# Two-layer attention stack on one NeuronCore: windowed attention moved from elementwise products on VectorE to banded matmuls on TensorE

## Chip, cores and metric

The kernel runs on one core of one Trainium2 chip. The metric is device time of the launch in microseconds (us). The kernel before takes 328.93 us, the median of two runs (328.53 and 329.33).

## What is computed

A residual stream x of 2048 tokens by 512 features (bf16) passes through four attention layers, A, B, A, B. Each is x = x + layer(layernorm(x)), with its own projections wqkv and wo; the two A layers share weights, and so do the two B layers. There are 32 heads of 16 features.

```python
# layer A: linear attention with a feature map
pq = einsum("bhsd,hdf->bhsf", q, w_phi); pk = einsum("bhsd,hdf->bhsf", k, w_phi)
phi_q = concat([softmax(pq), softmax(-pq)]); phi_k = concat([softmax(pk), softmax(-pk)])
kv = einsum("bhsf,bhsd->bhfd", phi_k, v);  z = einsum("bhsf->bhf", phi_k)
o = einsum("bhqf,bhfd->bhqd", phi_q, kv) / (einsum("bhqf,bhf->bhq", phi_q, z) + 1e-6)

# layer B: each token attends to 8 tokens of its past, 2 apart (offsets 0, 2, ..., 14)
W, dil = 8, 2
idx = pos[:, None] - (arange(W) * dil)[None, :];  mask = idx >= 0
logits = where(mask, einsum("bhsd,bhswd->bhsw", q, k[idx]) * 16 ** -0.5, -1e9)
o = einsum("bhsw,bhswd->bhsd", softmax(logits), v[idx])
```

## The kernel before

The tokens are worked in four blocks of 512 (b = 0..3), the two passes through A and B are L = 0 and 1. Stages of one (L, b) are Python methods that record small steps per engine: `s_a1` (keys, values and the kv sums of layer A), `s_a2` (queries of A), `s_a3` and `s_a4` (normalisation, output of A), `s_b1` (projections of B), `s_b2` (logits and softmax of B), `s_b3` (weighted values of B), `s_out` (output projection, residual and the next layernorm). The steps of all stages are then issued in one order written out by hand, the string `_ORDER`: each word names a thread (a stage on an engine) and takes its next step. `_CHOICE` says for each eviction of PSUM (the accumulator memory) and some others whether VectorE (DVE) or ScalarE (ACT) does it (`flex`, `copy`), and for each residual add whether DVE adds it or TensorE (PE) adds it with an identity matmul (L523) and ACT evicts (L530). `_SLOTS` gives each tile its buffer. So every engine runs a fixed queue; the DMAs are all issued by SyncE's (SP's) queue, also in that order. Each PSUM tile is one bank of 512 fp32 per partition, eight in all.

Layer B before works on features across partitions and tokens along the free axis. `prod` (L1019) multiplies Q, repeated eight times, by eight shifted windows of K: 128 by 4096 elements on DVE, four per (L, b). `lgt` (L1026) sums the 16 features of a head on PE with the 0/1 matrix `indQK`; PE takes four 32-column tiles side by side. Exp (L1033) and the denominator (`den` L1042 on PE, `rd` L1047 and L1049 on ACT) follow, then `pt` (L1054) on DVE. For the values, 16 DMAs per (L, b) copy shifted rows of V into `Vg` (L988). `pav` (L1081) multiplies them with the weights on DVE, 128 by 4096 elements, four per (L, b), and `mo` (L1090) sums them on PE with `indAV`.

Small copies of the last 16 tokens of K and V from block to block (L953, L965, L969) are on GpSimd (POOL). The `vaug` ones (L614) are there too.

PE runs in several array layouts: the whole array for projections (L520, L593, L605, L698, L927), column tiles of 32 or 64 for L1026, L1090, L714, L782 and L668, row tiles for L808, and sixteen 32x32 tiles for L900.

Of the kernel before, what the change touches and what calls it, by code (L numbers as in the profile page):

```python
# [8 lines left out]
BF16 = mybir.dt.bfloat16  # L9
# [20 lines left out]
KVW = 16 + TB  # L30
VGW = 3 * KVW + TB + 8
# [5 lines left out]
_BUFS = {"big": 8, "med": 16, "t2": 6, "ps": 8}  # L37
# [3 lines left out]
    "fold_dma": (),  # L41
    "half_k": ((0, 3), (1, 3)),
    "half_ln": (),
    "split": ((1, 2), (1, 3)),
    "v_dram": (),
    "half_mo": (),
    "rho_pad": 0,
# [10 lines left out]
av 8 i i i i i i i i i i i i 0 f 0 g e 2t 0 bs 9 h a d c 0 j k t i i j l 27 o p 3 3 d6 b 1x 1x t 1y o m 2 2 1q  # L58
1z 1x 1x q u t r 1q v x w n s 1r w 1s 4 20 y 21 1x 22 1x 23 1q 1q 1q 1q 1v 1w z 3d 3d 3d 1u 1t 25 3e 3e 3e z 5
3e 3e z z 26 10 18 18 d5 1 z 16 11 4i 15 6 1h 13 3d 3e 3e 25 25 26 18 25 18 12 26 26 28 26 26 26 26 19 12 28  # L60
2a 28 1h 18 14 12 12 1a 28 1c 3e 2g 2g 1f 2h 2h 1h 1h 1b 1i 2b 1b 1e 1d 29 2j 2k 1h 1j 1n 2r 1b 1l 2s 1b 2c 2r
1k 2s 17 2g 2g 2h 2h 1k 1k 2h 2h 2h 2h 2d 1g 2d 2d 2d 2e 2j 1m 35 36 32 2o 2o 33 2s 33 32 33 33 2r 2s 2s 1o 2o
2o 2d 2r 3a 1k 3a 1p 2p 2o 24 24 2s 24 2u 2v 35 37 2u 2u 2u 2s 2i 2w 2j 3a 2s 3a 2l 2z 2j 24 32 32 34 2m 3b 33
3d 3f 3f 2z 2z 2z 33 2f 33 33 2f 2f 2f 3a 3a 2q 2q 2q 30 3a 2n 3a 3a 2z 3e 2q 2x 35 35 b6 3b 3a 2y 31 31 31 31
3c 3c 38 3c 39 3c 3m 3f 3n 3o 3o 3o 24 24 3g 3g 3g 3f 3p 3q 3g 3g 3g 3g 3g 3r 3q 3f 3g 24 3h 3i 3i 5l 5m 5n 3p
3s 3q 3j 3k 3k 3t 3q 3p 3x 5m 3w 3u 3h 3i 3i 3q 3v 3q 3q 3y 3h 3i 3q 3i 3h 3i 3q 5l 5o 5p 5r 5m 5q 7 7 3z 3q
3i 3j 3k 5m 5l 5s 3k 7 7 5m 5m 5m 3h 3i 7g 40 5u 44 41 42 5t 5m 5m 3j 3j 7h 7i 3k 5v 5m 5w 43 7h 45 7j 45 60
3k 3k 3k 46 45 45 5y 5x 5z 61 61 48 47 47 61 49 47 4a 47 4b 62 47 4b 63 3j 4g 94 4c 45 4d 45 4e 4f 3k 45 45 61
64 63 4h 4p 65 95 7j 7j 66 4q 63 96 95 97 97 63 67 7h 63 67 69 7h 6b 4k 4k 4k 4l 4p 4r 4k 4m 4p 4p 4s 4t 7k 7n
6a 68 6c 4o 7m 50 50 4u 4u 4u 4n 4u 7l 4w 97 7o 7p 7p 7q 7s 3l 4x 7r 7r 7p 7t 7p 6o 7u 50 7r 7r 7v 6o 6j 4v 4y  # L70
4j 6o 6q 6o 4j 4z 6k 6p 6r 6j 7r 6e 6l 95 6d 95 7v 6t 6s 6f 6d 7w 6e 7z 7x 98 9b 9a 99 6g 7y 9c 6e 6j 6j 9d 9d
6u 9d 6e 6n 80 6m 9d 6h 6v 6v 9e 9h 9f 6i 9g 9f 6w 6v 6v 6w 6w 9f 9i 9f 87 88 8h 9j 9f 50 82 9j 9l 6w 6x 6x 87
87 6w 81 83 9n 6x 9k 87 8b 89 51 51 51 51 52 52 8c 8c 8e 6u 6u 6u 9m 8j 8a 8d 8c 6v 6y 3l 8f 82 9o 82 85 82 50
51 52 4z 4z 4z 9q 9q 9s 8c 6z 8g 6y 6z 9r 71 70 6y 6y 6z 6z 72 86 a0 a0 a1 73 84 8i 74 75 74 74 50 74 8i 76 8i
77 a2 76 79 53 53 54 55 54 a5 56 53 54 9v 78 76 9q 9q 76 a0 81 53 9v 9w 9p 7a 57 9v 9u a7 76 7a 9t 8j 7c 9y 54
58 59 59 59 9v 59 9x 7d 7e 5a 8j 8j 7b 7f 5c 5b 5d 5b 5b a0 8k 5e 5b 5f 8k 9z a7 5b 5f 5j 8k 8k 8l a3 5i b4 a4
b7 5h b4 b4 b4 8l 5g b5 b5 a7 b5 b5 a7 8k 8l 8j c3 8i c3 b8 c4 c4 c4 c4 a8 8m a8 a8 a8 c3 a9 a9 5k at c1 b5 a6
8m au au c1 c2 b5 c2 aw c2 c2 a8 a9 b5 b5 8n 8o 8n 8p 8m at au at at 8n 8q 8m a7 aa 8n aw 8r 8s au au au 8s 8s
8t au au 8s 8v a6 a6 8u aa 8w aa 8x 8u 8u 8u 8y ab ac ab ad a6 aa b7 8u b9 b7 c3 8y 90 92 c1 91 c1 c2 8z c2 c2
aw ay ab c2 ba ae ab af aw b0 c4 c4 b1 bc ag ag ag ag ah bc aj ak bc c1 c4 c4 bc al ax c3 ai ai ai bd b1 ai am  # L80
93 bf bi bg az bf ai am ar bf bf bg bg aq b7 bg bg bg bg bg bb an ao ag ag ap bi ag ag b1 b1 bc b2 c2 bi bn bi
bl bk as bq br br bq br br bq bq b1 br by by by by bt b3 b3 b3 b3 br be be be br br bz c5 c5 bh bj bn bn bn c5
bu c4 by by by by c6 bo by c6 c6 c5 bt bt bt bn bv c6 c6 c6 bz be bp bp bw bm bp bp c0 c0 by c6 c6 bx c0 c0 c9
c5 ca c6 cb cb cc cb cd ce cd fr fs c7 c8 c7 c8 c8 ft cc ci cf cd cg cd c7 c8 c8 fs fu c8 e2 fu ch cd e3 cd cc
cj ck e4 cd c7 c8 c8 c7 e3 e2 cm cd c8 e6 e7 fu cl cd cd cn cp co e5 e3 hb e3 cr e2 ea e9 cq hc cs e3 cs e8 e3
e3 hd eb ec e3 e3 e3 ed ct cv hc eh cs he ee cs ef cw eg ei cx ei ei cu ei cu cu cu fs cy fs fv ej cu cy d0 cz
ek d2 fw fx fz d3 cs cs fy cs cs g0 g0 g0 el ek em ek en ek d4 d1 dc g1 eo ek g2 g3 g2 dc de eo es g0 g4 dd dh
g2 g5 g2 he hc eq g6 d7 d8 d7 d7 d7 he di dc g2 dc d9 ep er hc et dn hf da db df dh dh dh hi hh hj hg hk hk hk
dj dk dl dm dm g6 g7 g9 dn dn dg ga f0 f0 hl hm hn hm ho hm ev ew f1 hk dn g8 do do hp f2 fa fc hm hq do do dp
ev ex fc gb ev f0 dp ey dn f3 f0 hm fc f4 hq ev ez fc do dp dn dq dq d6 f5 f6 dm dm eu hs gi gj gi fd gs hr fd  # L90
ht fd hu hv fd dq fe fe f5 f5 f8 f5 f9 f7 fb gk fd fe fc gn gn gp gi gi gl gm gd gd gd ge ic gf i7 i7 i9 gg i8
dr dr dt ds dr du hx hy gd dq gu dr dv gn gq gh i7 ff ia gu fb go ff fg fh fb fb eu gv gc gn i2 gr i3 hx hz hx
i7 i2 ib gv i4 hx i1 gc hw i2 i2 i5 gu i0 gu gv gv gw gt ie fg fi if i6 ie id gw if dw dx id gv gw id id ie ie
if if ig dw ff ig if ig fg fj dw e0 dw ff fg fk ie fl fm fl fn gu fl fl fp ih ih ih ih e1 ii ii ii ik ij fq dy
gt gt gt fo fo il io io io io ii im ip iq ip is ir ir ih ii in ip ip iu it ir gx ir gy gx gx gx gz gy h0 dz dz
iv gy h1 h4 gx gy h2 h4 iw iv h5 h5 h6 h7 gy h4 h3 h5 h8 h9 h7 h7 h4 h5 ha h7
# [4 lines left out]
    "0011111111111001110111111010000010010000000000000001011111101100100000110101000110000010000001110111"  # L101
    "1101011110010000110101000000000000001101011000000000100100000000000000000101111100000011011000000000"
    "0000000000001101111010000000100101011111010000011001110111000000000000000111111011101110010100101000"
    "00000000000001111001000000000000000000000000000000000000000000000000000000000001111"
)


_SLOTS = {
    "big": (
        "0123456701231231456204632073205712053720457604356704213560421356720415763215063506432506"  # L110
    ),
    "med": (
        "0123456789abcdef5837ae98eeaeae471853bc9e43cbe47199ce3185413cebf94c8f74e3581bc71931bc7f370bf9ac21584e"
        "af9c37214a0b589dec37"
    ),
    "t2": (
        "0123450123450342150132451032451032451032451302153421530421503452014520345123045130425123504321504321"
        "5043215043210451023134"
    ),
    "ps": (  # L120
# [9 lines left out]
class _Fast:  # L130

    def __init__(self, ctx, tc, A_x, A_wqkv, A_w_phi, A_wo, B_wqkv, B_wo, out):
# [16 lines left out]
        for n in ("xn", "xnT", "oT", "Eq", "rS", "kvp", "K", "QT", "Vg", "PT", "vh"):  # L149
            setattr(self, n, {})  # L150
# [1667 lines left out]
```

## Time and profile before

| what | value |
|---|---|
| device time, median of two runs | 328.93 us |
| span of the profiled execution, first to last instruction | 327.5 us |
| PE busy | 310.3 us (95%) |
| DVE busy | 302.2 us (92%) |
| ACT busy | 279.3 us (85%) |
| POOL busy | 25.3 us (8%) |
| granted PE clock | 0.998 |
| bytes moved by DMA | 35.41 MB |

The span is what one profiled execution shows between its first and last instruction; its own device time is not listed beside it, and the launch adds 1.4 us to the span when the median is taken for it (328.93 - 327.5). Matmuls overlap: a 128x512 matmul is listed with 380 ns while the next starts some 216 ns after it, so PE's busy time covers short pauses too. "PEld" is the loading of weights, which runs beside the matmuls. A group's line gives the source line, the engine, the operation, the tiles, the count, the busy time and the mean duration of one.

### The profile page before, as it was taken

Reading aid. Unit: us, or ns where it says so; the run is one execution under the profiler, and the core shown is the slowest. Engines: PE = TensorE matmul, PEld = TensorE weight load, DVE = VectorE, ACT = ScalarE, POOL = GpSimd, SP = SyncE. Lnnn points to the kernel's source line nnn. Section 1 sums busy time; section 2 is a strip of 40 time slices with the busy share of each in tenths; the row PEclk is TensorE's granted clock in tenths of the full one; section 3 lists DMA queues with packets and bytes.
Section 4 is the critical chain, followed back from the end, with each engine's and each line's share of the span. In section 5 each row is a group of like instructions: output and inputs, shape, how many; then the busy total and the mean of one; then the engine's idle time right before and its main releaser. Section 6 shows DMA issues by size and latency. Waiting matters only on the chain. (4 is left out here: it accounts for less than half of the span.)

```text
span 327.5 us, 8033 instructions
## 1 busy us (share of the span) xinstructions
PE 310.3 (95%) x3176; PEld 149.5 (46%) x3203; DVE 302.2 (92%) x439; ACT 279.3 (85%) x634; POOL 25.3 (8%) x50
## 2 busy tenths in 40 slices
PE   7999999999999999999999999979999999999873
PEld 3655456445444444443444455644544454433221
DVE  7998995998998999899999999699999999999993
ACT  5999988998888999989999999798999996676550
POOL 4000000000021003000000000000000208400000
PEclk9999999999999999999999999999999999999999
DMA  7980000004556899998750300023436977679952
GB/s 197 380 197 3 0 2 4 2 20 120 105 148 135 152 164 133 139 121 154 137 135 1 67 3 2 4 59 90 128 58 125 179 146 134 150 139 158 166 176 92
DMA packets 37388, 35.41 MB, mean 108 GB/s; under 512 B 23008, under 2 KB 32224, under 8 KB 37344
## 3 DMA queue, kind: packets, MB, share of 16 engines
q1 hardware_dynamic: 36816, 34.81, 53.6%
q8 instruction: 27, 0.44, 0.6%
q14 instruction: 17, 0.14, 0.2%
q10 hardware_dynamic: 528, 0.02, 0.1%
HBM read 10.50 MB, written 2.36 MB: 39 GB/s over the span
## 5 line engine op out<-in xcount | busy, mean ns | idle before, releaser
L927 PE MATMUL ps<-xnT,WB 128*128 128x512 bf16 x384 | 87.6, 380 | 0.5 <-DMA xnT<-xn 0.5
L1081 DVE TENSOR_TENSOR pav<-PT,Vg 128x4096 bf16<-128x4096 bf16 (+1 forms) x34 | 72.0, 2162 | 1.5 <-DMA Vg<-V 1.0
L1019 DVE TENSOR_TENSOR prod<-QT,K 128x4096 bf16<-128x4096 bf16 x32 | 72.5, 2291 | 0.3 <-ACT QT L192 0.2
L927 PEld LDWEIGHTS <-WB 128*128 128x128 bf16 x384 | 42.3, 114 | 43.3 <-issue 5.8
L520 PEld LDWEIGHTS <-oT 128*128 128x128 bf16 x256 | 23.8, 97 | 34.5 <-ACT oT L192 5.7
L192 ACT CAST oT<-ps 128x512 bf16<-128x512 f32 (+1 forms) x60 | 32.1, 587 | 8.4 <-PE ps L1090 7.1
L706 ACT ACTIVATE Eq<-ps 128x512 bf16<-128x512 f32 x64 | 34.0, 615 | 0.7 <-PE ps L698 0.6
L520 PE MATMUL ps<-WoB,oT 128*128 128x512 bf16 x122 | 32.1, 380 | 2.4 <-ACT oT L192 2.0
L599 ACT ACTIVATE Ek<-ps 128x512 bf16<-128x512 f32 x64 | 33.6, 622 | 0.4 <-PE ps L593 0.2
L698 PE MATMUL ps<-xnT,WA 128*128 128x512 bf16 x128 | 30.7, 380 | 0.6 <-DVE Eq L816 0.6
L540 ACT ACTIVATE sqd<-x 128x512 bf16<-128x512 bf16 x48 | 30.1, 643 | 1.0 <-DVE x L533 0.8
L605 PE MATMUL ps<-WA,xnT 128*128 128x512 bf16 x120 | 30.0, 380 | 0.5 <-issue 0.2
L593 PE MATMUL ps<-WA,xnT 128*128 128x512 bf16 x124 | 29.7, 380 | 0.6 <-DMA xnT<-xn 0.2
L520 PE MATMUL ps<-WoA,oT 128*128 128x512 bf16 x120 | 29.2, 380 | 0.4
L533 DVE SCALAR_TENSOR_TENSOR x<-ps,x 128x512 bf16<-128x512 f32 x38 | 25.4, 686 | 1.9 <-PE ps L520 1.7
L192 ACT CAST V<-ps 128x512 bf16<-128x512 f32 x31 | 17.5, 595 | 4.4 <-PE ps L927 4.3
L192 ACT CAST K<-ps 128x512 bf16<-128x512 f32 x31 | 17.8, 585 | 3.7 <-PE ps L927 3.3
L530 ACT ACTIVATE x<-ps 128x512 bf16<-128x512 f32 x26 | 15.1, 598 | 6.4 <-PE ps L523 6.3
L192 ACT CAST QT<-ps 128x512 bf16<-128x512 f32 x29 | 17.1, 592 | 2.5 <-PE ps L927 2.5
L651 DVE TENSOR_TENSOR Ek<-Ek,rk 128x4096 bf16<-128x4096 bf16 (+1 forms) x10 | 18.6, 1858 | 0.5 <-ACT rk L646 0.5
L593 PEld LDWEIGHTS <-xnT 128*128 128x128 bf16 x128 | 12.1, 97 | 15.4 <-DMA xnT<-xn 0.7
L446 ACT ACTIVATE xn<-x,nmr,rstd 128x512 bf16<-128x512 bf16 x23 | 18.2, 822 | 1.0 <-DVE nmr L435 0.8
(129 smaller groups left out, 433.3 us busy)
## 6 DMA issues: line engine op xcount, KB each, us to landing
Vg<-V SPq DMA_DIRECT2D x128, 131.5 KB, 4.4
Prho<-rd SPq DMA_DIRECT2D x8, 512.0 KB
x<-in_A_x_dram SPq DMA_DIRECT2D x3, 512.0 KB
WB<-in_B_wqkv_dram SPq DMA_DIRECT2D x3, 512.0 KB, 11.6
wraw<-in_A_wqkv_dram SPq DMA_DIRECT2D x4, 256.0 KB, 4.5
out_dram<-x SPq DMA_DIRECT2D x4, 256.0 KB, 2.2
out_dram<-x SPq DMA_DIRECT2D x8, 128.0 KB, 2.2
x<-in_A_x_dram SPq DMA_DIRECT2D x4, 128.0 KB
```

The costliest lines, as they stand in the source:

```text
L192: self.nc.scalar.copy(out=out, in_=in_)
L520: nc.tensor.matmul(y[:], lhsT=oT[:, c, t * P:(t + 1) * P], rhs=Wo()[:, c, :], start=(c == 0), stop=(c == NB - 1 and not onpe))
L533: nc.vector.scalar_tensor_tensor(out=xb[:, t, :], in0=T[t][:], scalar=1.0, in1=xb[:, t, :], op0=ALU.mult, op1=ALU.add, **kw)
L540: nc.scalar.activation(out=sqd[:], in_=xb[:, t, :], func=ACT.Square, accum_out=T["ss"][:, t:t + 1])
L593: nc.tensor.matmul(pk[:], lhsT=xnT[:, t, k, :], rhs=self.WA[:, k, D:2 * D], start=(k == 0), stop=(k == NB - 1))
L599: nc.scalar.activation(out=T["E"][:, t, s, :], in_=T["k", t][:], func=ACT.Exp, scale=1.0 - 2.0 * s)
L605: nc.tensor.matmul(pv[:], lhsT=xnT[:, t, k, :], rhs=self.WA[:, k, 2 * D:3 * D], start=(k == 0), stop=(k == NB - 1))
L698: nc.tensor.matmul(pq[:], lhsT=self.WA[:, k, hb * P:(hb + 1) * P], rhs=xnT[:, :, k, :], start=(k == 0), stop=(k == NB - 1))
L706: nc.scalar.activation(out=self.Eq[L, b][s][:, :, hb, :], in_=T[hb][:].rearrange("p (t i) -> p t i", t=4), func=ACT.Exp, scale=1.0 - 2.0 * s)
L927: nc.tensor.matmul(pp[:], lhsT=self.WB[:, k, i * D + c:(i + 1) * D:NB], rhs=xnT[:, :, k, :], start=(k == 0), stop=(k == NB - 1))
L1019: nc.vector.tensor_tensor(out=pr[:], in0=QT[:, c:c + 1, :].to_broadcast([P, NW, TB]), in1=win, op=ALU.mult)
L1081: nc.vector.tensor_tensor(out=pv, in0=PT[:, :, lo:lo + n].unsqueeze(1).to_broadcast([P, NB, 2, n]), in1=vw, op=ALU.mult)
```

## The change

K, Q, V of layer B get another layout, and its products and sums become matmuls over short bands of tokens. The tokens of a block are dealt out to partitions by parity, since the window's steps are 2: `xv` reads x as (block, parity r, half f, partition p), so each tile of 128 token rows holds tokens of one parity, and the window of 8 tokens becomes 8 neighbours in it.

- Q is evicted to `Qs` and scattered by eight DMAs per (L, b) into `Qbd`, in which every head pair stands block-diagonally (the rest is zero). V is projected with tokens on partitions, written to DRAM (`vwr`) and read back by eight DMAs per (L, b) into `Vbd` (`vrd`), where each group of 32 tokens has a copy with the heads block-diagonal. `Vg` and its 16 DMAs are gone.
- For each of four quarter blocks t, `sc` computes the scores of 32 keys against 40 queries of two heads per matmul (32x32 tiles, 80, 64 or 16 columns, 40 matmuls for each half f), `ex` takes the exponential of 128x640, `msk` multiplies by the band's 0/1 mask (128x1280 on DVE), `mo` makes the weighted sums (`pv`, 40, 32 or 8 columns) and the denominators (`dn`, 80, 64 or 16 columns) on 64x32 tiles, `ln` and `rd` invert the denominator on ACT, and `nrm` multiplies on DVE from PSUM into `oT`. In b = 0 the first quarter of each parity (t = 0 and 2) has no matmuls for the keys before it in `pv` and `dn`.
- Layer A takes PSUM banks in pairs (`pp`): exponentials, the eviction of `oT` and the products `mulp` work on 1024 columns in place of 512; the copies `bs` of the broadcast rho are gone.
- `_ORDER`, `_CHOICE` and `_SLOTS` are new. Identity matmuls for the residual go from 26 to 4. POOL zeroes `Qbd` and `Vbd` once at the start (four memsets of 4096 or 4608 elements per partition, ahead of the `vaug` ones) and its copies from block to block are gone.

```diff
+    def pp(self):
+        return self.psp.tile([P, 2, TB], F32, name="pp", tag=self.slot("pp"))
...
-        xv = self.A_x.rearrange("b (j p) d -> p (b j) d", p=P)
+        xv = self.A_x.rearrange("b (k f p r) d -> p (b k) r f d", f=2, p=P, r=2)
...
-            nc.scalar.activation(out=T["E"][:, t, s, :], in_=T["k", t][:], func=ACT.Exp, scale=1.0 - 2.0 * s)
+            nc.scalar.activation(out=T["E"][:, 2 * t:2 * t + 2, s, :], in_=T["k", t][:], func=ACT.Exp,
+                                 scale=1.0 - 2.0 * s)
...
-        def prod(c):
-            K, QT = self.K[L, b], self.QT[L, b]
-            T["p", c] = pr = self.big([NW, TB], "prod")
...
-        def pav(q, lo=0, n=TB):
-            Vg, PT = self.Vg[L, b], self.PT[L, b]
...
+        def qsc(r, o):
+            lo = 32 * r + DH * o
+            nc.sync.dma_start(out=self.Qbd[b % 2][lo:lo + DH, :, o, :], in_=T[0][lo:lo + DH, :, :])
+
+        def vwr(r):
...
+            dst = self.VD[L][r, 256 * b:256 * b + 256, :].rearrange("(f p) d -> p f d", p=P)
+            nc.sync.dma_start(out=dst, in_=T[2][:, 2 * r:2 * r + 2, :])
+
+        def vrd(r, c):
+            j = 0 if b else 1
+            src = self.VD[L][r, 256 * b - 32 + 32 * j:256 * b + 256, c * P:(c + 1) * P]
+            lo = c % 2 * DH
+            dst = self.Vbd[b % 2][32 * c:32 * c + 32, r, j:9, lo:lo + DH, :].rearrange("k j d e -> k j (d e)")
+            nc.sync.dma_start(out=dst, in_=src.rearrange("(j k) e -> k j e", k=32))
...
+        def mm(S, r, c, s, n, pos, K, k0, q0):
+            o = S[32 * c:32 * c + 32, r % 2, s * 80 + pos:s * 80 + pos + 1]
+            out = bass.AP(o.tensor, o.offset, [list(o.ap[0]), [WN, 2], [1, n]])
+            nc.tensor.matmul(out, lhsT=K[32 * r:32 * r + 32, c, k0:k0 + 32],
+                             rhs=Q[32 * r:32 * r + 32, c, :, q0:q0 + n],
+                             start=(s == 0), stop=(pos == 32), tile_position=(32 * r, 32 * c),
+                             skip_group_check=True)
+
+        def sc(f):
+            S = T[f] = self.pp()
+            K = self.K[L, b]
+            for s in range(4):
+                for c in range(NB):
+                    for r in (2 * f, 2 * f + 1):
+                        mm(S, r, c, s, WN if s < 3 else 32, 0, K, t * P + 32 * s, t * P + 32 * s)
...
+            for c in range(NB):
+                for r in (2 * f, 2 * f + 1):
+                    mm(S, r, c, 3, 8, 32, Kp, k0, t * P)
+
+        def ex(f):
...
+            nc.scalar.activation(out=E, in_=T[f][:, :, 0:320], func=ACT.Exp, scale=float(DH) ** -0.5,
+                                 accum_out=self.stE[:, 2 * idx + f:2 * idx + f + 1])
 
         def msk():
+            E = self.ET[L, b, t][:].rearrange("p f i s o q -> p (f i s o) q")
+            nc.vector.tensor_tensor(out=E, in0=E, in1=self.maskW[:].unsqueeze(1).to_broadcast([P, 32, WN]),
+                                    op=ALU.mult)
...
+        def pv(s, n, pos, q0):
+            E, O = self.ET[L, b, t], T["O"]
+            for i in range(2):
+                for cc in range(2):
+                    for f in range(2):
+                        for o in range(2):
+                            u = 2 * f + (cc if o == 0 else 1 - cc)
+                            e = 4 * f + 2 * i + o
+                            nc.tensor.matmul(O[32 * u:32 * u + 32, o, i * P + q0:i * P + q0 + n],
+                                             lhsT=V[64 * cc:64 * cc + 64, t // 2, s, :, e],
+                                             rhs=E[64 * cc:64 * cc + 64, f, i, (s + 3 - 4 * (t % 2)) % 4, o, pos:pos + n],
+                                             start=(q0 == 0 and pos == 0 and i == 0), stop=False,
+                                             tile_position=(64 * cc, 32 * u), skip_group_check=True)
+
+        def dn(s, n, pos, q0, last):
+            E, O = self.ET[L, b, t], T["O"]
+            for cc in range(2):
+                for f in range(2):
+                    for o in range(2):
+                        u = 2 * f + (cc if o == 0 else 1 - cc)
+                        w = O[32 * u:32 * u + 32, o, 256 + q0:257 + q0]
...
+                        nc.tensor.matmul(out, lhsT=self.oneB[64 * cc:64 * cc + 64, :, :],
+                                         rhs=E[64 * cc:64 * cc + 64, f, :, s, o, pos:pos + n],
+                                         start=False, stop=last,
+                                         tile_position=(64 * cc, 32 * u), skip_group_check=True)
...
+        def ln():
+            T["l"] = self.t2([2, 256], "lnd", F32)
+            nc.scalar.activation(out=T["l"][:], in_=T["O"][:, :, 256:512], func=ACT.Ln, bias=self.tiny_t[:, 0:1])
 
         def rd():
+            T["r"] = self.t2([2, 256], "rden")
+            nc.scalar.activation(out=T["r"][:], in_=T["l"][:], func=ACT.Exp, scale=-1.0,
                                  accum_out=self.stR[:, idx:idx + 1])
 
+        def nrm():
...
+            out = self.oT[key, b][:, :, t * P:(t + 1) * P].rearrange("p (i o) q -> p o i q", o=2)
+            nc.vector.tensor_tensor(out=out, in0=T["O"][:, :, 0:256].rearrange("p o (i q) -> p o i q", i=2),
+                                    in1=T["r"][:].rearrange("p o (i q) -> p o i q", i=2), op=ALU.mult)
...
+                for t in range(4):
+                    self.s_b2(L, b, t)
+                    self.s_b3(L, b, t)
+                self.s_out("b4_%d%d" % (L, b), "A%d" % (L + 1), b, lambda: self.WoB, L == 1)
```

Instructions per engine in the built programs, on the path that runs (the matmul rows count matmuls; each has a weight load beside it):

| | before | after |
|---|---|---|
| `prod` and `pav` on DVE, 128x4096 | 62 (and 4 of 2048) | 0 |
| `lgt`, `mo`, `den` on PE | 544 | 0 |
| `sc` on PE | 0 | 2560 |
| `pv` and `dn` on PE | 0 | 2496 and 1248 |
| changes of PE's array layout | 109 | 157 |
| all PE instructions | 6408 | 17884 |
| B's Q, K, V evictions: DVE, ACT | 5, 91 | 60, 36 |
| residual adds on DVE; identity matmuls with ACT | 38; 26 | 60; 4 |
| `ex` on ACT | 16 of 512 columns | 64 of 640 |
| `ln` and `rd` on ACT, 512 columns | 8 and 8 | 32 and 32 |
| V and Q transfers on SP | 128 | 64 (`qsc`), 16 (`vwr`), 64 (`vrd`) |

## The prediction

> **What bounds the kernel now.** I read the page first: span, busy shares, then its costliest groups and the instruction queue.
>
> ```profile
> span 327.5 us, 8033 instructions
> PE 310.3 (95%) x3176; PEld 149.5 (46%) x3203; DVE 302.2 (92%) x439; ACT 279.3 (85%) x634; POOL 25.3 (8%) x50
> q8 instruction: 27, 0.44, 0.6%
> ...
> L927 PE MATMUL ps<-xnT,WB 128*128 128x512 bf16 x384 | 87.6, 380 | 0.5 <-DMA xnT<-xn 0.5
> L1081 DVE TENSOR_TENSOR pav<-PT,Vg 128x4096 bf16<-128x4096 bf16 (+1 forms) x34 | 72.0, 2162 | 1.5 <-DMA Vg<-V 1.0
> L1019 DVE TENSOR_TENSOR prod<-QT,K 128x4096 bf16<-128x4096 bf16 x32 | 72.5, 2291 | 0.3 <-ACT QT L192 0.2
> ```
>
> PE and DVE are both over 90% and ACT is not far off. The two products of layer B are 144.5 of DVE's 302.2 us. An average hides stages, so next the busy time by stretch.
>
> ```profile
> 20.00:50.00 30.00, 29.68 (x313) 15.59 (x315) 27.77 (x48) 28.07 (x61) 0.77 (x2) 1.00 0.10 22
> 110.00:140.00 30.00, 29.90 (x209) 13.71 (x212) 28.60 (x24) 27.55 (x65) 3.04 (x3) 1.00 1.02 144
> 290.00:328.00 38.00, 27.50 (x225) 9.69 (x221) 31.93 (x29) 18.27 (x40) 0.00 (x0) 0.98 0.76 147
> ```
>
> The columns are the length, then busy us of PE, PEld, DVE, ACT, POOL, then clock, DMA share and GB/s. In the middle PE is full (29.90 of 30). Only in the last 37.5 us does it pause for 10.0, with DVE the busiest engine. So taking work from DVE gains little by itself; what counts is whether PE's queue becomes shorter. For that I read PE's timeline.
>
> ```profile
> 50.25 2.15 PE L668 MATMUL ps<-Ek,vaug 128*33 128x64 bf16 x128
> 52.33 1.04 PE L698 MATMUL ps<-xnT,WA 128*128 128x512 bf16 x4
> ...
> 67.18 1.24 PE L698 MATMUL ps<-xnT,WA 128*128 128x512 bf16 x5
> 68.35 0.65 PE L900 MATMUL ps<-Eq,R 32*32 32x512 bf16 x32
> 68.94 1.04 PE L520 MATMUL ps<-WoA,oT 128*128 128x512 bf16 x3
> ...
> 68.35 0.19 PEld L900 LDWEIGHTS <-R 32*32 32x32 bf16 x32 [0.42 <-issue]
> ```
>
> Four prices. A matmul of 512 columns costs (1.24 - 0.38) / 4 = 0.215 us. A change of array layout: the last L698 starts at 67.18 + 0.86 = 68.04, L900 at 68.35, 0.31 later, so the change costs 0.095. Sixteen 32x32 tiles run together: 32 matmuls of 512 columns take 0.59, two rounds of 0.215, the change and a little. Dispatch: 32 weight loads, 88 ns each, lie within 0.19, so one pair of load and matmul leaves every (0.19 - 0.088) / 31 = 3.3 ns. The slowest pace of a small pair is L668's, 64 columns on two tiles: (2.08 - 0.095) / 128 = 15.5 ns. Last, the groups by form:
>
> ```profile
> L533 DVE SCALAR_TENSOR_TENSOR x<-ps,x 128x512 bf16<-128x512 f32 x38 | 25.4, 686 | 1.9 <-PE ps L520 1.7
> L1026 PE MATMUL ps<-prod,indQK 128*32 128x512 bf16 x256 | 16.4, 381 | 1.7 <-DVE prod L1019 1.7
> L1090 PE MATMUL ps<-pav,indAV 128*32 128x512 bf16 x240 | 16.1, 382 | 1.2 <-DVE pav L1081 1.1
> L816 DVE TENSOR_TENSOR Eq<-ps,Eq 128x512 bf16<-128x512 f32 x25 | 16.1, 682 | 0.1
> L1033 ACT ACTIVATE E<-ps 128x512 bf16<-128x512 f32 x16 | 9.5, 601 | 1.2 <-PE ps L1026 1.2
> L1047 ACT ACTIVATE lnd<-ps,tiny_t 128x512 f32<-128x512 f32 x8 | 5.6, 702 | 0.7 <-PE ps L1042 0.6
> L1049 ACT ACTIVATE rden<-lnd 128x512 bf16<-128x512 f32 x8 | 5.1, 631 | 0.3
> L1042 PE MATMUL ps<-E,indDen 128*128 128x512 bf16 x15 | 4.5, 379 | 0.0
> L1033 ACT ACTIVATION_READ_ACCUMULATOR E<-ps 128x1 f32 x16 | 3.4, 210 | 0.0
> ```
>
> **PE, which decides.** Removed: L1026, 256 matmuls four abreast, 64 x 0.215 = 13.8; L1090, 60 x 0.215 and 8 of half size, 13.8; L1042, 16 x 0.215 = 3.4; 22 identity matmuls, 4.7. Together 35.7. The projections stay at 384 matmuls. Layout changes go from 109 to 157: 48 x 0.095 = 4.6 more.
>
> New: 6304 small pairs, which the trace doesn't show. From below, eight tiles at a time: a round of `sc` costs 80/512 x 0.215 = 0.034, one of 64 columns 0.027, and where the columns are fewer, eight dispatches, 0.026. An `sc` call (3 x 0.034 + 0.027 + 0.026) is 0.155, times 64 is 9.9. A `mo` is ten rounds of 0.026 for `pv` and 0.155 for `dn`, 0.415, times 32 is 13. The low end is 23. From above, L668's pace: 6304 x 15.5 ns = 98. By form they are nearest to L900 (tiled in rows and columns), but 3.3 ns is shown for only 32 pairs in a row, and a `mo` has 120; I take 27 (4.3 ns a pair). PE's queue changes by 27 + 4.6 - 35.7 = -4.1 us.
>
> **DVE.** It loses `prod` and `pav` (144.5), `pt` 5.4 and the old mask 0.3. It gains `msk`: the adds of layer A (L630, L626) go from 687 ns at 1024 elements to 1217 at 2048, so 1280 cost 0.82, times 32 is 26; `nrm` like L816, 32 x 0.68 = 22; 55 more Q, K, V evictions at 0.686, 38; 22 more residual adds at 0.77, 17; ten `vaug` copies 7; wider `oT` copies 4.5, eight xn 3. Sum about 269.
>
> **ACT.** Gone: 55 evictions 31, `oT` copies 23, residual adds 15, `bs` 4, ten `vaug` and eight xn 12. Layer A's wide exponentials: 256 to 512 columns cost 0.23 more in the eviction rows (374 to 602), so 512 more cost 0.46 over the 0.53 that the 128 old ones average, 64 x 0.99 = 63 against 67.6, 5 less. New: `ex` of 640 is 0.71 + 0.21, times 64 is 59 against 12.9, +46; `ln` 24 x 0.70 and `rd` 24 x 0.82, +37. Sum about 272. Both engines get 15% of slack, so all that hides under PE.
>
> **Waits.** The paused 10.0 us at the end hold 5.3 after the last matmul (ends 322.2), which stays: last add, store. The other 4.7 are waits for `pav`, `prod` and the evictions behind them. After the change the end has its own chain: ACT needs 2 x 0.92 + 0.70 + 0.82 = 3.4 per quarter, 13.5 for the last four, while PE has some 10 us of outputs and bands to put between. I take 4 us saved over the whole kernel; the bounds are 0 and the 10.6 that PE idles between its first and last matmul (17.2 less 1.3 and 5.3).
>
> **Moved and new waits.** On SP each `vrd` waits until its `vwr` has landed (the similar rho write lands in 3.0 us), and behind it stand `qsc`, the transposes of xn and stores, for which the projections L593, L605 and L927 wait. Cover: the K and Q projections of the block, 32 x 0.215 = 6.9 us, and its exponentials, 7.4 on ACT. Without it, 16 x 3 = 48 us. The 128 `Vg` transfers make room for 144 smaller ones. POOL's four zero fills, by 198 ns at 128 and 311 at 256 elements some 4 us each, hold up the `vaug` ones until about 18 us; the first L668 is at 46.4. The pairing of banks leaves four slots; a pair fills in 8 x 0.215 = 1.7 us and is read in 2 x 0.99, which PE covers with other work. All these I cost at nothing.
>
> **Sum.** 327.5 - 4.1 - 4 = 319.4 span; the median of the runs is 1.4 above the span, so 320.8 us.
>
> **Rivals.**
> 1. Supply (slower). An instruction queue packet took 0.006 x 16 x 327.5 / 27 = 1.16 us and carried 0.44 MB / 27, some 256 of PE's 6408 instructions. The band groups have 12,608 instructions: if PE outruns what lies ready, they go at 1.16 per 256, 57 us in place of 27, and the end is 349.4 + 1.4 = 350.8. It decides against the change from 6.6 ns a pair (42 us) on. For it: a `mo` with 240 instructions in 0.4 us is denser than anything before. Against: on average a page lasts over 4 us, and L668's 256 instructions ran at its column pace.
> 2. Short matmuls don't overlap and go at L668's pace: 98, so 327.5 + 98 - 31.1 - 4 + 1.4 = 392. Against it, L900's overlap. The Trainium skill ("TensorE: Matmul & The Clock Gate", section "Wait — 56ns, not 53.3ns?") states that matmuls never start closer than about 25 ns however few columns; per instruction that would make 158 us of the pairs, an estimate. L668's 15.5 ns already lies under it, so the trace bears it out at most per tile.
> 3. The two row halves of `pv` and `dn` write the same bank and take turns. Each round of eight becomes two of four: in `pv` 2 x 17 ns of columns, ten times 34, in `dn` 3 x 68 + 54 + 26, together 0.62 in place of 0.415 per `mo`, 0.21 x 32 = 6.7 us more: 327.5. Every row-tiled form before (L808, L900) writes one bank per row tile, so nothing shows it. The Trainium skill ("TensorEngine Tiling (Array Packing)", section "Gotcha 1: PSUM Pressure") says that row tiles can't use one bank at the same time; no run here shows that yet.
> 4. The chain per quarter (PE, ACT, DVE, PE, ACT twice, DVE, PE) brings as many waits as go and costs 3 us: 327.8.
> 5. Lighter DVE and ACT free nearly all of PE's 10.6: 314.
>
> **How the numbers follow.** Forecast 58% (own range 315 to 326), supply 11%, L668's pace 5%, shared banks 10%, new waits 10%, all waits gone 6%. A measurement of this kernel tells about 2% from no change, which is 322.4 to 335.5. Faster: three quarters of the forecast and rival 5, 0.50. Slower: rivals 1 and 2 and the far tail of 3 and 4, 0.20. Same 0.30. The range reaches from between rival 5 and the forecast, 311, to most of the supply case, 345.
>
> **What would show it.** Right: PE's start-to-start in `sc` and `mo` near 4 ns a pair, an `sc` call of some 0.16 us and a `mo` of 0.42; DVE and ACT near 270; PE over 93% busy until the last 20 us. Wrong: pairs at 7 ns or more, or idle PE with "issue" as its cause inside a `mo` (rivals 1 to 3); PE idle behind `ex`, `rd` or `nrm` in the middle (rival 4); PE waiting for `Vbd`, `Qbd` or xnT (the SP queue).

## Result and the profile after: 466.3 us, slower by 42%

The changed kernel takes 466.31 us (median; 465.47 to 467.15) against 328.93 before: ratio 1.416, 95% interval 1.405 to 1.426. The time lies far outside the forecast (320.8) and its range, and beyond both rivals that pointed this way, the supply of instructions (350.8) and L668's pace (392). Some executions of a kernel are slower as a whole, at a lower clock, so where a kernel's executions lie far apart the shorter ones are compared. The page first:

```profile
span 463.7 us, 19566 instructions
PE 364.9 (79%) x8888; PEld 197.5 (43%) x8941; DVE 312.8 (67%) x519; ACT 292.9 (63%) x573; POOL 19.9 (4%) x33
PEclk9899996997699987989897589878997899998776
q8 instruction: 71, 1.16, 1.1%
...
L198 DVE CAST Vs<-ps 128x512 bf16<-128x512 f32 x22 | 53.5, 2483 | 6.2 <-PE ps L922 6.2
```

No engine is full any more: PE pauses for 99 us of the span (463.7 - 364.9). Its granted clock, 0.998 before, is 0.880 on average. The instruction queue carries 71 packets in place of 27, and an eviction of V on DVE lasts 2483 ns on average. By stretch, with the columns as before (length; busy us of PE, PEld, DVE, ACT, POOL; clock, DMA share, GB/s):

```profile
0.00:20.00 20.00, 11.51 (x83) 7.44 (x85) 16.46 (x27) 7.44 (x15) 18.42 (x29) 0.91 0.89 270
200.00:300.00 100.00, 81.03 (x2087) 45.59 (x2095) 63.87 (x106) 67.83 (x129) 0.68 (x2) 0.85 0.18 39
400.00:464.00 64.00, 41.15 (x1679) 23.72 (x1688) 29.73 (x44) 29.15 (x61) 0.00 (x0) 0.82 0.24 63
```

PE pauses at the start, in the middle and at the end alike. So it isn't one late transfer. What PE waits for, as the waits of PE have it (us in total, times, longest):

```profile
PE pp L1037 <- issue: 22.8, 14, 2.7
PE pp L982 <- issue: 11.0, 7, 4.2
PE pp L1051 <- issue: 6.3, 5, 2.1
```

These three lines are the bands (L982 `sc`, L1037 `pv`, L1051 `dn`), and "issue" says that PE waited for nothing that the profile shows, no other engine and no transfer of data: 40 us, which I read as time in which PE had no instruction (some 10 us of "issue" more stand before other lines). PE's timeline shows it inside one `sc` and inside one `mo`:

```profile
109.87 0.84 PE L982 MATMUL pp<-Qbd,K 32*32 32x80 bf16 x80
110.63 1.04 PE L804 MATMUL ps<-Eq,ZM 128*32 128x128 bf16 x32
111.61 0.31 PE L982 MATMUL pp<-Qbd,K 32*32 32x80 bf16 x10
116.15 0.79 PE L982 MATMUL pp<-Qbd,K 32*32 32x80 bf16 x70 [4.23 <-issue]
...
129.11 0.46 PE L1037 MATMUL pp<-et,Vbd 64*32 64x40 bf16 x28
132.05 0.63 PE L1037 MATMUL pp<-et,Vbd 64*32 64x40 bf16 x52 [2.48 <-issue]
```

Ten matmuls of an `sc`, a hole of 4.23 us, and the other seventy; 28 of a `mo`, a hole of 2.48, and the other 52. Where there is no hole, 80 `sc` matmuls take 110.63 - 109.87 = 0.76 us with a layout change, 8.3 ns a pair without it (0.095), not 4.3.

### The profile page after: what moved, and what is told of

Its sections match the earlier page's. It is cut to its first block, busy times and chain, and to the rows that moved or that the text cites. A ratio compares the mean times of both kernels' runs of the same rounds, so it can differ in the third digit from the quotient of the medians.

```text
span 463.7 us, 19566 instructions
## 1 busy us (share of the span) xinstructions
PE 364.9 (79%) x8888; PEld 197.5 (43%) x8941; DVE 312.8 (67%) x519; ACT 292.9 (63%) x573; POOL 19.9 (4%) x33
## 3 DMA queue, kind: packets, MB, share of 16 engines
q8 instruction: 71, 1.16, 1.1%
## 4 chain that ended last, share of the span: by engine, by line
PE 56%; issue 13%; DVE 13%; ACT 11%; DMA 4%; SPq 1%; DVEq 0%; ACTq 0%
PE ps L535 11%; PE ps L915 10%; PE pp L1037 6%; PE pp L601 5%; PE ps L614 5%; PE ps L922 4%; PE pp L714 4%; PE pp L982 3%; DVE Vs L198 3%; ACT Vs L200 3%; DVE xn L459 3%; PE pp L1051 2%; PE ps L680 2%; DMA Qbd<-Qs 2%; DVE x L548 2%
## 5 line engine op out<-in xcount | busy, mean ns | idle before, releaser
L915 PE MATMUL ps<-xnT,WB 128*128 128x512 bf16 x256 | 67.9, 406 | 6.6 <-ACT Vs L200 3.1
L1008 ACT ACTIVATE et<-pp 128x640 bf16<-128x640 f32 x64 | 45.6, 718 | 26.2 <-PE pp L982 25.9
L198 DVE CAST Vs<-ps 128x512 bf16<-128x512 f32 x22 | 53.5, 2483 | 6.2 <-PE ps L922 6.2
L1037 PE MATMUL pp<-et,Vbd 64*32 64x40 bf16 (+2 forms) x2496 | 31.5, 219 | 23.7 <-issue 22.8
L982 PE MATMUL pp<-Qbd,K 32*32 32x80 bf16 (+2 forms) x2560 | 29.8, 203 | 19.9 <-issue 11.0
L535 PEld LDWEIGHTS <-oT 128*128 128x128 bf16 x256 | 26.0, 110 | 41.0 <-issue 18.2
L1037 PEld LDWEIGHTS <-Vbd 64*32 64x32 bf16 x2496 | 27.4, 140 | 35.0 <-issue 33.5
L915 PEld LDWEIGHTS <-WB 128*128 128x128 bf16 x256 | 24.8, 102 | 37.5 <-issue 14.5
L982 PEld LDWEIGHTS <-K 32*32 32x32 bf16 x2560 | 24.1, 92 | 35.8 <-issue 31.1
L535 PE MATMUL ps<-WoA,oT 128*128 128x512 bf16 x120 | 35.7, 445 | 3.6 <-ACT oT L200 1.3
L922 PE MATMUL ps<-WB,xnT 128*128 128x512 bf16 x110 | 30.7, 399 | 5.1 <-issue 2.6
L722 ACT ACTIVATE Eq<-pp 128x1024 bf16<-128x1024 f32 x32 | 31.0, 1024 | 3.6 <-PE pp L714 3.5
L607 ACT ACTIVATE Ek<-pp 128x1024 bf16<-128x1024 f32 x32 | 31.1, 1042 | 3.2 <-PE pp L601 3.1
L614 PE MATMUL ps<-WA,xnT 128*128 128x512 bf16 x123 | 31.3, 389 | 0.5 <-issue 0.3
L601 PE MATMUL pp<-WA,xnT 128*128 128x512 bf16 x123 | 30.4, 391 | 1.0 <-ACT Eq L722 0.6
L714 PE MATMUL pp<-xnT,WA 128*128 128x512 bf16 x128 | 29.6, 379 | 0.0
```

Source lines behind the costliest of these rows:

```text
L198: self.nc.vector.tensor_copy(out=out, in_=in_)
L535: nc.tensor.matmul(y[:], lhsT=oT[:, c, t * P:(t + 1) * P], rhs=Wo()[:, c, :], start=(c == 0), stop=(c == NB - 1 and not onpe))
L601: nc.tensor.matmul(pk, lhsT=xnT[:, t, k, :], rhs=self.WA[:, k, D:2 * D], start=(k == 0), stop=(k == NB - 1))
L607: nc.scalar.activation(out=T["E"][:, 2 * t:2 * t + 2, s, :], in_=T["k", t][:], func=ACT.Exp, scale=1.0 - 2.0 * s)
L614: nc.tensor.matmul(pv[:], lhsT=xnT[:, t, k, :], rhs=self.WA[:, k, 2 * D:3 * D], start=(k == 0), stop=(k == NB - 1))
L714: nc.tensor.matmul(pq, lhsT=self.WA[:, k, hb * P:(hb + 1) * P], rhs=xnT[:, :, k, :], start=(k == 0), stop=(k == NB - 1))
```

## Experiments

The theory after this reading has several parts. Instructions reach PE too slowly for the bands ("supply"), each pair costs about 8 ns even when it is there ("dispatch"), the eviction of V got slow by its write order, POOL's zero fills hold up DVE, and the new order brings waits. Each experiment takes one of them away or isolates it.

**The pace of small pairs alone.** A kernel with nothing but PE work: stretches of 1536 pairs on 32x32 tiles, of 16 and of 80 columns, between full matmuls, then 16 times 96 pairs and 16 full matmuls.

> Not the attention: PE alone. 64 full matmuls of 512 columns, 1536 pairs of weight load and matmul on sixteen 32x32 tiles with 16 columns, 64 full ones, 1536 such pairs with 80 columns, 64 full ones, then sixteen times 96 pairs of 80 columns and 16 full ones; the output is a copy of x. Theory instruction supply: the first 250 or so pairs of a long section leave at some 8 ns, then 256 instructions per 3.7 us, 29 ns a pair, with steps visible; a section of 1536 takes 38 us or so with either width, and the last part runs without gaps, as its 224 instructions per round come with 3.4 us of full matmuls. Theory dispatch: 1536 x 8.3 ns = 13 us per section without steps. Theory column pace (what the forecast took): 16 columns 3.3 to 4.3 ns a pair, 5 to 7 us; 80 columns 4.3.

PE's timeline and the instruction queue:

```profile
25.31 1.43 PE L32 MATMUL pk<-w 32*32 32x16 bf16 x159
29.11 1.17 PE L32 MATMUL pk<-w 32*32 32x16 bf16 x128 [2.37 <-issue]
32.84 1.19 PE L32 MATMUL pk<-w 32*32 32x16 bf16 x128 [2.56 <-issue]
...
141.11 0.96 PE L32 MATMUL pk<-w 32*32 32x80 bf16 x96
142.00 3.63 PE L27 MATMUL full<-w 128*128 128x512 bf16 x16
145.55 0.96 PE L32 MATMUL pk<-w 32*32 32x80 bf16 x96
...
q8 instruction: 39, 0.64, 1.2%
```

This is the clearest view of the case. Once the first 159 or 223 are gone, the pairs come in packs of exactly 128, which are 256 instructions, one pack every 3.45 to 4.00 us, 3.7 on average (3.73 here, 32.84 - 29.11), about a microsecond of work and 2.5 of nothing. The windows show the two stretches as alike, for 16 columns (first) and for 80 (second):

```profile
25.00:67.00 42.00, 14.24 (x1521) 12.95 (x1519) 0.00 (x0) 0.00 (x0) 0.57 0.02 4
83.00:125.00 42.00, 15.61 (x1538) 13.30 (x1536) 0.00 (x0) 0.00 (x0) 0.57 0.02 4
```

(There is no ACT in this kernel: after PE, PEld and DVE comes POOL.) Columns don't matter, the instruction does. The queue's packet lasts about 1 us (39 packets, 1.2% of 16 engines' 213.8 us: 1.05 each), so the period isn't the transfer's time; it lies between transfers. The single records of the trace show what it is made of. The packet behind the pack that runs from 29.11 to 30.30 us starts at 30.25 and lands at 31.46, and the next pack starts at 32.84. So it goes all along both stretches: a packet starts as a pack runs out (from 0.3 us before its end to 0.5 behind it), and the next pack begins 1.3 to 1.6 us after the landing. Nothing is fetched ahead there. Three holes of the changed kernel, the two shown above and one at 120.12, end in the same way, 1.4 to 1.5 us after a packet landed (114.62, 130.60 and 118.67 us). With 96 pairs to 16 full matmuls (224 instructions in 4.44 us) there is no hole: supply keeps up.

A pack itself takes some 8 ns a pair, and not evenly: its first 32 pairs start 3.3 to 3.8 ns apart, those from the 65th on 8.3 to 8.5 (averages over 32 pairs), at 16 columns and at 80. And where PE is served in this way, the granted clock falls to 0.57. The full matmuls behind each stretch show the price: their first nine or ten starts are some 427 ns apart, the later ones 216.

**More and fewer instructions in the changed kernel.** First the denominators of a quarter issued twice (the first four `dn` calls), which is 2048 instructions, 8 pages of 256:

```diff
+            for s in range(4):
+                dn(s, WN if s < 3 else 32, 0, 32 * s, False)
             for s in range(4):
                 dn(s, WN if s < 3 else 32, 0, 32 * s, s == 3 and not halo)
```

> The changed kernel with the main denominator matmuls issued twice (the denominators are doubled but for the halo, so the output differs): 1024 pairs, 2048 PE instructions more. Theory instruction supply: eight pages more, most of them in starved stretches, 20 to 30 us more, 486 to 496. Theory dispatch: 1024 x 8.3 ns = 8.5 us more, 475.

504.08 us, ratio 1.530 (1.526 to 1.534). Its three shorter executions, 502.5 to 504.9, are 36 to 39 above the changed kernel, 4.5 to 4.8 per page. That is more than either theory gave (20 to 30, and 8.5 for the dispatch of 1024 pairs). It is far nearer to supply; the clock fell with it, to 0.838, and what that adds was not separated. The hole moved to where the pairs were added:

```profile
PE pp L1051 <- issue: 25.6, 13, 3.0
```

Then the denominators in 24 matmuls per `mo` in place of 40 (one access pattern over four bands), 1024 instructions fewer:

> The changed kernel with the denominators in 24 matmuls per quarter block in place of 40 (256, 48 and 16 columns): 512 pairs, 1024 PE instructions fewer, same result, more columns each. Theory instruction supply (256 instructions per some 3.7 us where PE outruns it): four pages fewer, up to 15 us less, 451 to 458. Theory dispatch (each pair 8.3 ns, the gaps have other causes): 512 x 8.3 ns = 4 us less, eaten by the wider columns: 463 to 467.

462.29 us, ratio 1.394 (1.386 to 1.402), single executions from 457 to 467. That is 4 less, with a scatter as large, and outside the 451 to 458 that supply gave: inconclusive by itself.

**The eviction of V.** The changed kernel writes `Vs` with the features of a head strided, every element 16 bytes from the last. Here the write is dense and the read from PSUM is what it then has to be:

```diff
-                self.copy(dve, dst[:, c, :].rearrange("p (a d e) -> p a e d", a=NB, d=DH),
-                          T[i, c][:].rearrange("p (a e d) -> p a e d", a=NB, d=DH))
+                self.copy(dve, dst[:, c, :].rearrange("p (a d e) -> p a d e", a=NB, d=DH),
+                          T[i, c][:].rearrange("p (a e d) -> p a d e", a=NB, d=DH))
```

> The changed kernel with one edit: V's eviction writes its bf16 output densely and reads PSUM in strides, in place of a dense read and a write every 16 bytes. The result is the same. Changed kernel: 466.3 us, its 32 V evictions take 2.48 us each. Theory scattered write: the eviction falls to some 0.7 us, and as PE's V matmuls wait for its PSUM slots and the values are late for the weighted sums, the time falls by half or more of 32 x 1.8 = 57 us, to 410 to 437. Theory instruction supply: PE is held by its queue of instructions, which stays as long; evictions get short but the time falls by less than 15 us, to 451 or more.

The groups by form of this kernel:

```profile
L198 DVE CAST Vs<-ps 128x512 bf16<-128x512 f32 x22 | 14.9, 686 | 8.2 <-PE ps L922 8.2
L200 ACT CAST Vs<-ps 128x512 bf16<-128x512 f32 x10 | 5.7, 581 | 2.1 <-PE ps L922 2.1
```

686 ns on DVE in place of 2483, 581 on ACT in place of 2482; DVE is at 276.9 us and ACT at 275.7, near the 269 and 272 that were forecast. The time is 448.55 (440.65 to 449.52), 18 to 26 less. That lies between the ranges of the two theories (410 to 437, and 451 or more). The reads from PSUM are now the strided ones and cost nothing that shows; the write order was the price.

**POOL's zero fills.** In the changed kernel's first microseconds DVE's timeline has two normalisations, of one tile each, and this operation costs 0.41 us in the trace of before (L444 there):

```profile
6.26 3.78 DVE L459 TENSOR_SCALAR xn<-x,rstd,nmr 128x512 bf16<-128x512 bf16 x1
...
10.14 3.93 DVE L459 TENSOR_SCALAR xn<-x,rstd,nmr 128x512 bf16<-128x512 bf16 x1
```

POOL's fills (3.5 to 4.1 us each) run from 2.93 to 17.9 us, and each of these two operations ends 0.15 us after a fill does. The fills in pieces of 512 and 256 elements:

```diff
-            nc.gpsimd.memset(self.Qbd[i][:], 0.0)
+            for c in range(NB):
+                for o in range(2):
+                    nc.gpsimd.memset(self.Qbd[i][:, c, o, :], 0.0)
...
```

> The changed kernel with only the zero fills on POOL in pieces of 512 elements in place of 4096 and 4608. Same result. Theory shared access of POOL and DVE to memory: the two early layernorm instructions on DVE that took 3.78 and 3.93 us in place of 0.41 take under 1 us, and the end comes 5 to 7 us earlier, 459 to 461. Rival: the start has room, or the fills hold DVE up as long in pieces: no change, 464 to 468.

460.11 us (456.6 to 463.3), ratio 1.394 (1.387 to 1.402): 6 less, and the two tiles took 0.66 and 0.51.

**Three mends together**: dense V, merged denominators, small fills.

> The changed kernel with V's dense eviction, the 24 denominator matmuls, and the zero fills on POOL in pieces of 512 elements (they hold up VectorE's first layernorm by two times 3.4 us). Same result. From 466: V's eviction took 18 off, the denominators some 4, the pieces should give back 5 to 7: 437 to 443. Theory instruction supply: no less than 430, since 16,860 PE instructions stay. Theory that evictions and the start hold the kernel: the gains add up beyond their parts, 420 or less.

444.15 us, ratio 1.345 (1.338 to 1.351). These three give 22 of the 137 us lost, less than the 28 that their parts add up to and just short of the 437 to 443 expected.

**The pairs.** Now about the same columns in 1280 pairs in place of 6304: per `sc` one matmul of 320 columns for each of eight tiles (2560 in all, as before), per `mo` 16 of 128 and 8 of 256 (2048 each, against 2560), with dense V and small fills. In the second kernel only the bands are wide.

```diff
+                    nc.tensor.matmul(S[32 * c:32 * c + 32, r % 2, 0:320], lhsT=K[32 * r:32 * r + 32, c, k0:k0 + 32],
+                                     rhs=Q[32 * r:32 * r + 32, c, :, q0:q0 + 160], start=True, stop=True,
...
+                            nc.tensor.matmul(O[32 * u:32 * u + 32, o, i * P:i * P + P],
+                                             lhsT=V[64 * cc:64 * cc + 64, t // 2, j, :, e],
+                                             rhs=E[64 * cc:64 * cc + 64, f, i, :, o, 0:32],
...
```

> The columns of the bands stay, their instructions go: each sc call has 8 matmuls of 320 columns with one group of keys (in place of 40 with the keys' own), the weighted sums 16 of 128 columns, the denominators 8 of 256: 1280 pairs in place of 6304, so the scores and sums are not the reference's. With V's dense eviction and the small zero fills. ACT, DVE and DMA do the same work as in the changed kernel. PE then has 7,840 instructions, 31 pages. Theory instruction supply: the pauses named issue inside the bands vanish, PE's clock comes back, and the time falls by 80 us or more, to 320 to 360. Theory that the new order, the chain per quarter or the DMAs of Q and V hold it: PE waits for ACT, DVE or DMA in place of its instructions, 400 or more.

> The changed kernel with only its band matmuls made wide as described for the wide bands (1280 pairs in place of 6304, scores and sums not the reference's); V's scattered eviction and the long zero fills stay. Theory instruction supply as the larger cause: 360 to 390, that is V's eviction costs 20 to 40 more than in the kernel with the dense one, as it is no longer hidden behind PE's pauses. Theory that V's eviction is the larger cause: above 420.

Wide bands alone: 398.66 us, ratio 1.209 (1.204 to 1.214), 68 less than the changed kernel, at a clock of 0.932. That is above the 360 to 390 expected and well below 420: the pairs are the larger cause, and not all of it. With dense V and small fills: 361.16, ratio 1.094 (1.089 to 1.100), 37.5 less again and just over the 320 to 360 that supply gave. The page of the latter:

```profile
span 357.9 us, 9580 instructions
PE 312.7 (87%) x3878; PEld 147.1 (41%) x3917; DVE 267.0 (75%) x519; ACT 272.4 (76%) x573; POOL 21.9 (6%) x81
q8 instruction: 33, 0.54, 0.7%
```

No "issue" wait of bands is left in PE's waits, DVE and ACT are where the forecast had them, and it is still 31 above the 329.91 of before beside it and 40 above the forecast. PE pauses for 45 us where it paused for 17. Its waits name many places:

```profile
PE ps L310 <- DVE mask L272: 4.4, 1, 4.4
PE pp L894 <- DVE Eq L843: 3.8, 5, 1.2
PE pp L997 <- DMA Qbd<-Qs: 3.4, 4, 2.0
PE pp L997 <- ACT et L1005: 3.3, 10, 0.9
PE pp L836 <- DVE rho L829: 2.7, 2, 1.6
PE ps L919 <- DMA xnT<-xn: 2.3, 1, 2.3
PE pp L1063 <- DMA Vbd<-vd: 2.1, 2, 1.9
```

This kernel also answers the rival of the shared banks, for wide bands. Here is a `mo` in its timeline that does not wait, and nor does what follows it:

```profile
112.96 0.36 PE L1063 MATMUL pp<-et,Vbd 64*32 64x128 bf16 x16
113.13 0.30 PE L1072 MATMUL pp<-et,oneB 64*32 64x256 bf16 x8
113.36 1.90 PE L919 MATMUL ps<-xnT,WB 128*128 128x512 bf16 x8
```

From its first matmul to the next projection it takes 0.40 us, the change of layout (0.095) in it. With all eight tiles at once the columns make two rounds of 0.054 and one of 0.107, 0.31 with the change; if row halves on one bank took turns, it would be 0.52 at least. So they don't take turns here.

**What holds the wide kernel.** Three tries on it: without the transfers of Q into `Qbd` and of V through DRAM into `Vbd` (`qsc`, `vwr`, `vrd` empty), with layer A's product (`mulp`) not reading its PSUM pair, and both.

> The wide-band kernel (361.2 us) without the scatter of Q into Qbd and the way of V through DRAM into Vbd: the 64 + 16 + 64 transfers are left out and both tiles stay zero, so layer B's numbers are not the reference's. In the wide-band kernel PE waits 5.5 us on these two tiles (3.4 for Qbd, 2.1 for Vbd) and 3.0 on transposes of xn that stand behind them in SP's queue. Theory 'moves': these waits are on the path, and the clock that falls with them costs about as much again: 347 to 353 us. Rival 'other chain': the rest of the loss sits in the paired banks and the quarter's chain, and PE would wait for those instead: 358 to 361 us.

> The wide-band kernel with the products of layer A (mulp) multiplying Eq with itself in place of the PSUM pair of broadcast rho: PE's broadcasts stay, their pairs come free at once, and the sixteen products get shorter (both operands bf16 in SBUF). Layer A's output is not the reference's. In the wide-band kernel PE waits 5.8 us for these products (2.0 before L836, 3.8 before L894), and the stretch from 60 to 80 us has PE busy for 13.8 us at a clock of 0.74. Theory 'paired banks': waits plus the clock: 350 to 354 us. Rival 'other chain': PE finds the next wait (rho, oT, Qbd) right behind: 358 to 361 us.

> Both edits in one kernel: no moves of Q and V, and the products of layer A without the PSUM pair (outputs not the reference's). If the two kinds of wait add up: 336 to 346 us. If the per-quarter chain of exponential, mask, logarithm and product is what holds PE: over 352 us. Either way what is left above 329 belongs to the new order, the later start (first matmul 3.2 us later) and the remaining chain.

359.56, 370.43 (365.90 to 372.21) and 358.80 us. Taken at their word, nothing helped. But their traces start otherwise. First the wide kernel's DVE, then that of the kernel without the moves, which has the same instructions up to here:

```profile
6.24 0.61 DVE L463 TENSOR_SCALAR xn<-x,rstd,nmr 128x512 bf16<-128x512 bf16 x1
```

```profile
6.31 14.31 DVE L463 TENSOR_SCALAR xn<-x,rstd,nmr 128x512 bf16<-128x512 bf16 x1
```

14.31 us for an operation of 0.41: it ends at 20.62, when POOL has done its 52 fills and the four `vaug` ones behind them (20.5 us). The small fills had not removed the conflict: in these traces DVE either got in between two of them or waited for all (14.38 and 14.65 us in the other two kernels); what decides it stays open. The first L684 comes at 53.5 us in place of 42.7 (53.7 and 54.1 in the other two), so these three kernels carry some 10.8 us or a little more that have nothing to do with their edits. The comparison was worthless as it stood, and only the timeline of the first microseconds told so. The next three kernels have the tiles zeroed by four DMAs behind the last weight load:

```diff
+                for i in range(2):
+                    nc.sync.dma_start(out=self.Qbd[i][:].rearrange("p c o t -> p (c o) t"),
+                                      in_=z.to_broadcast([P, 8, TB]))
...
```

> The wide-band kernel with Qbd and Vbd zeroed by four DMAs from a zero tile behind the last weight load (about 25 us, where the DMA engines are idle) and not by POOL. In the trace of the kernel without moves one xn on DVE took 14.31 us beside POOL's 52 small memsets, against 0.61 in the wide-band kernel with the same start, and the first L684 came at 53.5 us, against 42.7. Theory 'port': POOL's fills hold DVE up by chance, so without them the start is as in the better of the two and the time is 358 to 362. Rival 'no port': something else was late in that execution, and nothing here changes the first xn: it still takes long in some.

> The kernel without the moves of Q and V, with the same filling by DMA (layer B's numbers are not the reference's). Theory 'moves' with the start taken out: 346 to 351 us, ten below the kernel with POOL's fills. Rival 'other chain': 357 to 361 us.

> As the one before, and the sums mo read a constant tile in place of the masked exponentials, so that PE doesn't wait there for ACT's exponential and DVE's mask of the quarter (both still run; layer B's numbers are not the reference's). If the chain per quarter holds PE: 336 to 344 us. If it doesn't: within 2 us of the kernel before it, and what is left above 329 is the new order and the clock that falls in its pauses.

361.47 us (ratio 1.096, 1.092 to 1.100), 350.12 (1.064, 1.058 to 1.070) and 351.71 (1.066, 1.061 to 1.072). In the first and second of them each xn up to 20 us takes at most 0.41. The moves of Q and V cost 361.47 - 350.12 = 11.3 us, as their theory had it (346 to 351). The wait of `mo` for the quarter's exponentials and mask costs nothing that shows (351.71 is 1.6 more, inside the scatter). That is one link of the quarter's chain. PE's waits for a pair of banks that `ex` or `nrm` holds stay in both kernels and were not tried, and so does a wait for a transpose, with no moves in the queue. In the kernel without the moves:

```profile
PE pp L994 <- ACT et L1002: 3.2, 11, 0.4
PE pp L1060 <- DVE oT L1086: 1.6, 5, 0.5
PE ps L924 <- DMA xnT<-xn: 1.9, 1, 1.9
```

With 10.8 taken off, the two shorter executions of the kernel with the unread pairs (365.90 and 368.74) are at 355.1 and 357.9 against 361.2, and the kernel with both edits is at 348.0 against 350.1: some 2 to 6 us for the paired products, by arithmetic and not by a run of its own.

Some 20 us over the kernel before are left at 350.12. Its windows show where PE pauses and where the clock is low:

```profile
0.00:20.00 20.00, 15.12 (x119) 8.78 (x120) 12.54 (x37) 11.62 (x23) 3.78 (x26) 1.00 0.89 275
60.00:80.00 20.00, 14.03 (x226) 6.71 (x225) 11.45 (x23) 10.80 (x24) 0.00 (x0) 0.74 0.01 2
200.00:260.00 60.00, 52.10 (x895) 27.34 (x888) 45.91 (x87) 45.66 (x97) 0.69 (x2) 0.91 0.11 29
```

At the start PE is busy for 15.1 of 20 us (18.2 before): its first matmul reads kvT, which DVE now zeroes at 4.1 us, behind an operation that waits for the load of w_phi (0.94 before). From 60 to 80 us the first block's rho, its products and `oT` follow each other with nothing put between, and PE is busy for 14.0 (19.7 before) at a clock of 0.74. How much of the 20 us is the order and how much the clock that falls in its pauses was not separated.

## Why the prediction was wrong, step by step

Taken off in the order of the runs, the 137 us divide into 68 for the pairs, 37.5 for V's write order and the fills, 11.3 for the moves and some 20 for the rest. In another order the shares would differ.

- **The price of the pairs is the step that failed.** The prediction took 6304 x 4.3 ns = 27 us. The pace alone, some 8 ns, makes 50; the holes on the three band lines add 40. Taking the pairs down to 1280 gave 68 us back, clock included. The 4.3 leaned on L900's 32 weight loads at 3.3 ns. They stood behind a wait of 0.42 us, and in the kernel of pairs alone exactly the first 32 pairs of a pack leave at such a pace (3.3 to 3.8 ns), the later ones at 8.3. So they show how fast instructions that have gathered leave, not how fast they follow for long. The text named 32 in a row as its weakness and took the low number all the same, though by its own sum the change gains nothing from 5.6 ns on and is 2% slower from 6.6.
- **Supply was the right rival at a wrong price.** It priced a page by its packet, 1.16 us, as if packets followed each other. They don't: where PE was starved a page came every 3.73 us, its packet starting only as the pack before ran out. At that rate 12,608 band instructions need 184 us of supply, and the 40 us of holes are what the wide matmuls between could not cover. The trace of before held this number: around L668's 256 pairs its instruction packets came at 47.54, 51.35 and 55.10 us, and only one pair of them in the whole kernel was closer than 3.6. "On average a page lasts over 4 us" stood against the rival; with a page every 3.7 it is no cover, since a stretch that is denser for longer than what lies ready (159 and 223 pairs in the kernel of pairs alone) runs dry. The Trainium skill ("Runtime: NRT & Kernel Launch", section "Instruction fetch mechanics") calls crossing a page mostly hidden; it is, for the 224 instructions in 4.44 us, and it is not for pairs alone.
- **The eviction of V** was priced by its shape, 0.686. Its write stride made it 2.48, on DVE and ACT alike: 32 x 1.8 = 58 us of engine time, 18 to 26 of device time. The rest of both engines' sums held: DVE 267 for 269, ACT 272 for 272. The Trainium skill ("SBUF — State Buffer", section "Door 1: The DMA port swizzle") has lines of 16 bytes in SBUF and a penalty for each access that goes to a new one; every element of `Vs` did, and this case's traces agree and give the price, 3.6 times the duration on DVE (2483 for 686 ns) and 4.3 on ACT (2482 for 581).
- **POOL's fills** were said to hold up only the `vaug` ones. They held up DVE's xn, and the start with it: 6 us. The Trainium skill ("SBUF — State Buffer", section "Who interferes with whom") says that DVE and POOL share a port pair under an exclusive lock. The traces agree, and go further than one instruction: 14.31 us across 52 fills.
- **The moves on SP**, costed at nothing under 6.9 us of projections, cost 11.3. In the kernel with the fills by DMA PE waits 4.7 us for `Qbd` and 2.3 for `Vbd`; what makes up the rest of the 11.3 stays open. The transposes of xn, which the prediction feared for behind the moves, were late by 1.9 us without them too.
- **Waits** were to fall by 4 us. PE paused for 45 in the wide kernel, against 17. The rival on the chain per quarter is in part answered: the wait of `mo` for exponentials and mask is worth nothing, and the waits for pairs of banks (3.2 and 1.6 us) were not tried. What the sum left out is that the order had been full before (19.7 of 20 at 60 to 80) and isn't now.
- **The removed work** (35.7 us of PE) did go, but PE is busy for 312.5 us in the best of the wide kernels, where the forecast has some 295 for it (310.3 - 35.7 + 4.6 + about 16 for the wide bands). The clock is of the right size for the difference, which is as much as the traces show: 0.95 in place of 0.998 over 313 us is 15. The sum took the durations of a PE that never rests for one that does; the projections on L915 take 406 ns in the changed kernel (0.880), where those on L927 took 380 before (0.998).
- **The two row halves that share a bank** don't take turns in the wide kernel (0.40 us for a `mo`, where turns would make 0.52). In the changed kernel nothing shows it either way: at 8 ns a pair, dispatch covers what turns would cost.

## What to carry to other kernels

Before work is cut into small matmuls, count instructions per microsecond in the densest stage and hold them against the pace that the trace shows for pages, their period and not their packet's duration; here 256 instructions per 3.7 us, and 8 ns per pair where they lie ready. Price an eviction by its write stride, and an idle engine's long operations by the engine that they hold up; then look at the first microseconds of every variant's timeline before two variants are compared. Behind a starved stretch PE ran slower here (nine or ten matmuls at 427 ns in place of 216), so pauses cost more than their length.

## What the hardware showed that was not expected

- Instructions come to PE in packs of 256 every 3.7 us once it outruns them, while their packets last about 1 us; the next packet starts only as the pack before runs out.
- Of small pairs that lie ready the first 32 start 3.3 to 3.8 ns apart, the later ones 8.3 to 8.5, at 16 columns and at 80.
- The granted clock falls with such pauses: 0.57 where PE was busy a third of the time, 0.880 over the changed kernel.
- A bf16 write with 16 bytes between elements took 2.48 us in place of 0.69 (DVE) and 0.58 (ACT).
- One DVE operation of 0.41 us lasted 14.31 beside 52 short fills on POOL, and 0.61 in another build with the same instructions up to there.
- Eight tiles in two row halves that write the same two banks ran their columns at once: 0.40 us for a `mo` of the wide kernel.
